# Two transfers instead of three for each half tile of keys and queries, and the second keys asked for one section later

## The chip, the cores and the metric

The kernel runs on one core of one Trainium2 chip. The metric is the time of one execution on the device in microseconds, the median of several runs. The core's engines are named as in the profile: PE (TensorE, matrix multiply; PEld is its loading of stationary operands), DVE (VectorE), ACT (ScalarE), POOL (GpSimd) and SP (SyncE, which here issues every DMA). Sixteen DMA engines move the data.

## The reference

```python
xn = layernorm(x)                                # 2048 tokens x 576
q, k, v = split(xn @ wqkv)                       # 32 heads of 18
s = softmax(q @ k.T * 18 ** -0.5) @ v            # for each head
s = concat_heads(s) @ wo
g = silu((gelu(xn @ w_gate) * (xn @ w_up)) @ w_down)   # 4608 inner
out = x + s * g
```

All inputs and outputs are 32-bit floats.

## The kernel before

A factor of a product is held as two parts, a rounded high part and the rest as a low part, and a product is the sum of high × high, high × low and low × high. For the attention scores these three products are laid one under the other in the contraction: a head has 18 rows, so 3 × 18 = 54 rows (`MROW`) of a half tile of 64 partitions (`HR`) hold the parts of one head of the keys, and another tile the matching parts of the queries. Row order for keys is high, low, high; for queries it is high, high, low. The remaining ten rows carry ones on the key side and, on the query side, zeros (`zq`) and two rows with the negated row maximum (`q<-mr`), so that the same matmul subtracts it.

The work runs in three parts.

1. The prologue normalizes and transposes the tokens, projects them with `wqkv` and stores both parts of the projected queries and keys in DRAM, in `qk[part, feature, token]`.
2. The middle runs 137 sections, nine of a first stage (`FIRST`) and 128 of attention. A section is one step of the gated network: 27 pairs of matmuls for gate and up (`pg`, `pu`, line 388) on 128 inner columns for a block of 512 tokens; every second section is followed by the down products (`py`, line 426). Between these pairs stand the matmuls of attention: `max_mm` (line 698) computes scores for the row maxima, `score_mm` (line 729) computes them once more for the exponential, and `values` (line 764) multiplies with the values. The order on PE is written out by hand; the other engines' order is planned when the program is built, by dependences and priority, except for what is wrapped in `tc.keep_in_program_order`, which stays in order.
3. The epilogue runs seven more sections and the last output projection.

A slot is one `max_mm` or `score_mm` step for two heads. A unit (`u`) is four heads and 512 queries, and takes four sections of eight slots. The maxima run 40 slots (five sections) ahead of the scores. The token block of the gated network changes every 36 sections, with loads of `xd`.

The loads that matter here, all issued by SP in one order:

- `load_k(n)` loads the chunk `n` of keys, 512 tokens of four heads: two tiles (`r`) of two half tiles (`a`), at line 662. There are seven buffers (`KB`). In the attention stage, a chunk is asked for in each section and first read one section later by `max_mm`.
- `load_q(u)` loads a unit's queries, also four half tiles (line 687), and ten rows of `zq` for each (line 688).
- `load_gu` (line 114) loads the gate and up weights of the next section into one of two buffers `raw`; POOL cuts them into parts `wh` and `wl` (lines 94 and 96), three pieces for each section, with five buffers. The next load into the same buffer waits for this.
- line 472 loads down weights (into `raw`, or `pT` in the first stage), which become `dh` and `dl`. POOL, or in the first stage ACT and POOL, also cuts the activation into `hh` and `hl` (lines 100 and 101 there).
- `load_o` (lines 529 and 530) loads finished attention outputs `OT` and the reciprocal sums `den` for up to seven heads at once; the source of `den` is m heads, each repeated over 18 rows.

In the first stage chunk `c` of keys is asked for as soon as the slots done, plus eight, reach its first slot; before the change that begins after the second section (n = 1), and chunk 1 is then asked for at once. Its first use is slot 8, in the fourth section (n = 3).

Of the kernel before, what the change touches and what calls it, by code (L numbers as in the profile page):

```python
# [16 lines left out]
S, D, H, DH, F = 2048, 576, 32, 18, 4608  # L17
# [15 lines left out]
SLOTS = 8  # L33
NA = NS // SLOTS
VC = NT // NA
KB, VB = 7, 2
# [6 lines left out]
MROW = 3 * DH  # L43
# [8 lines left out]
def f(ap):  # L52
    return ap.bitcast(F32)
# [13 lines left out]
def kernel(ctx: ExitStack, tc: tile.TileContext, x, wqkv, wo, w_gate, w_up, w_down, out):  # L67
    nc = tc.nc
# [8 lines left out]
    qk = dram.tile([2, 2 * D, S], F32, name="qk")  # L77
# [378 lines left out]
    def section(specials=(), tag="f", raw_d=None, early=None):  # L456

        n = FF["n"]
        FF["n"] += 1
        b, r = divmod(n // G, NR)  # L460
        g = n % G
        pairs, pg, pu = gate_up(tag)
        if g == 0:
            FF["hs"] = []
        keep = tc.keep_in_program_order if n == NU * NA + len(FIRST) + 1 else lambda i: i
        nxt = load_gu((n + 1) % (NR * G), keep) if n + 1 < NF else None
        if nxt:
            for k in range(NG - 1):
                split_gu(nxt, k)
        if g == G - 1:  # L470
            raw = FF["rawd"] = raw_d() if raw_d else raw_tile([P, G, D])
            nc.sync.dma_start(raw, w_down[r * G * P:(r + 1) * G * P, :].rearrange("(g p) n -> p g n", p=P))
            if early:
                FF["wd"] = early(raw)
        for p in spread(pairs, specials):
            p()
        if nxt:
            split_gu(nxt, NG - 1)
        FF["w"] = nxt
        if n + 1 < NF and (n + 1) % (NR * G) == 0:  # L480
            FF["xd"] = load_xd(b + 1)
        FF["act"] = activate(pg, pu, n < ATT.stop)

    def downs():
        while FF["down"] and (FF["down"][0][-1] < FF["n"] or FF["n"] == NF):
            down(*FF["down"].pop(0)[:-1])
            if FF["down"] and FF["gates"]:
                gates()

    def finish(pool=ffn, cut=split, bufs=1):  # L490

        n = FF["n"] - 1
        b, r = divmod(n // G, NR)
        hh = ffn.tile([P, TB], F32R, name="hh", bufs=G + 1)
        hl = ffn.tile([P, TB], F32R, name="hl", bufs=G + 1)
        cut(hh, hl, FF["act"])
        FF["hs"].append((hh, hl))
        if n % G == G - 1:
            wd = FF.pop("wd", None)
            if not wd:  # L500
                wd = [pool.tile([P, G, D], F32R, name=m, bufs=bufs) for m in ("dh", "dl")]
                cut(*wd, FF["rawd"])
            for h in range(2):
                once = n in ATT and n + G in ATT and r != NR - 2
                FF["down"].append((b, r, FF["hs"], wd, FF["Y"], (2 * h, 2 * h + 1), n + 1 + (0 if once else h)))
# [101 lines left out]
    for b in range(NB):  # L607
# [14 lines left out]
        for i in range(GROUPS):  # L622
            n = first + i * (1 if last else G)
# [17 lines left out]
    with tc.tile_pool(name="att", bufs=1, reuse_waits="tile") as att:  # L641
# [8 lines left out]
        def load_k(n, keep=lambda i: i, rs=(0, 1)):  # L650

            u, c = divmod(n, NA)
            if u >= NU:
                return
            cols = slice(c * TB, (c + 1) * TB)
            for r in rs:
                for a in range(2):
                    kk = f(KS[n % KB][r])[64 * a:64 * a + MROW, :]
                    h = QD * (u % NQ) + 2 * r + a
                    rows = slice(D + h * DH, D + (h + 1) * DH)  # L660
                    for n_, i in enumerate((0, 1, 0)):
                        keep(nc.sync.dma_start(kk[n_ * DH:(n_ + 1) * DH, :], qk[i, rows, cols]))

        def load_v(n):

            u, c = divmod(n, NA)
            if u < NU:
                g = u % NQ
                nc.sync.dma_start(VS[n % VB][:, 0:VC * VW].rearrange("p (t x) -> p t x", x=VW),
                                  vs[c * TB:(c + 1) * TB, QD * g:QD * (g + 1), :].rearrange("(t p) h d -> p t (h d)", p=P))  # L670
# [6 lines left out]
        def load_q(u, rs=(0, 1)):  # L677
            j, g = divmod(u, NQ)
            cols = slice(j * TB, (j + 1) * TB)
            for r in rs:  # L680
                t = QS[u, r] = att.tile([P, TB], F32R, name=f"q{r}", bufs=3)
                for a in range(2):
                    q = f(t)[HR * a:HR * a + MROW, :]
                    h = QD * g + 2 * r + a
                    rows = slice(h * DH, (h + 1) * DH)
                    for n, i in enumerate((0, 0, 1)):
                        nc.sync.dma_start(q[n * DH:(n + 1) * DH, :], qk[i, rows, cols])
                    nc.sync.dma_start(f(t)[HR * a + MROW:HR * a + HR, :], zq)

        def max_mm(u, i, a):  # L690
# [10 lines left out]
        def max_neg(u, keep=lambda i: i):  # L701

            nm = att.tile([P, 4 * QD], F32, name="nm", bufs=1)
            keep(nc.vector.tensor_reduce(nm, MX[u].rearrange("p a t c -> p (a t) c"), axis=AX.X, op=ALU.max, negate=True))
            m2 = NM[u] = att.tile([P, 2, 4 * QD], F32R, name="m2", bufs=2)
            nc.vector.tensor_copy(m2[:, 0], nm)  # L706
            nc.vector.tensor_tensor(m2[:, 1], nm, f(m2)[:, 0], op=ALU.subtract)

        def max_end(u):

            pm = ps.tile([P, P], F32, name="pm", tag="m", bufs=3)
            nc.tensor.matmul(pm[0:8 * QD, 0:P], NM.pop(u).rearrange("p i c -> p (i c)"), identr, start=True, stop=True)  # L712
            mr = att.tile([8 * QD, P], F32, name="mr", bufs=1)
            nc.vector.tensor_copy(mr, pm[0:8 * QD, 0:P])
            for a in range(QD):
                for i in range(2):
                    row = 64 * (a % 2) + MROW + i
                    c = 4 * (i * QD + a)
                    nc.sync.dma_start(f(QS[u, a // 2])[row:row + 1, :], mr[c:c + 4, :])
# [12 lines left out]
        def lead_pair(s):  # L732

            for a in range(2):
                max_mm(*divmod(s, NS), a)
# [66 lines left out]
        for r in range(2):  # L802
            load_k(0, rs=(r,))
            load_q(0, (r,))
        slot, chunk = 0, 1
        for n, m in enumerate(FIRST):
            none = [lambda: None]
            lead = [lambda s=s: lead_pair(s) for s in range(slot, slot + m)]
            if 0 in NM:
                lead.insert(1, lambda: max_end(0))  # L810
            section((n == 2) * 5 * none + lead + (m > 0 and n != 2) * none, "s" if n == 1 else "f", lead_raw)
            if slot + m >= NS > slot:
                max_neg(0, tc.keep_in_program_order)
            slot += m
            while n > 0 and chunk < KB and chunk * SLOTS <= slot + SLOTS:
                load_k(chunk, tc.keep_in_program_order)
                chunk += 1
            if n == 3:
                load_q(1)
            if n >= len(FIRST) - 2:  # L820
                load_v(n - len(FIRST) + 2)
            downs()
            finish(cut=split_ap)
        for n in range(NU * NA):
            u, i = divmod(n, NA)
            s0 = n * SLOTS
            section([p for s in range(s0, s0 + SLOTS) for p in slot_pairs(s)])
            if n > 0:
                load_k(n - 1 + KB)
            if i == 1 and u + 2 < NU:  # L830
                load_q(u + 2)
            gates()
            if n == NA:
                nc.gpsimd.memset(OT, 0.0)
                nc.gpsimd.memset(f(OW[1])[HR:P, KT, :], 0.0)
            tasks(n, 0)
            um, im = divmod(s0 + LEAD + SLOTS, NS)
            if im == 0 and um <= NU:
                max_neg(um - 1)
            for kt in range(i * SLOTS // 2, (i + 1) * SLOTS // 2):  # L840
                values(u, kt)
            load_v(n + 2)
            if im == 0 and um <= NU:
                max_end(um - 1)
            tasks(n, 1)
            downs()
            tasks(n, 2)
            finish()


    with tc.tile_pool(name="epi", bufs=1, reuse_waits="tile") as epi:
# [4 lines left out]
        n = NU * NA  # L856
# [78 lines left out]
```

## Time and profile before

| | |
|---|---|
| median of 3 runs | 2585.47 us (2585.27 to 2585.91) |
| profiled execution | 2584.62 us |
| its span, first to last instruction | 2582.7 us |
| PE, DVE, ACT, POOL busy | 100%, 78%, 58%, 54% of the span |
| DMA packets, bytes | 394912 packets, 326.93 MB, mean 127 GB/s |
| granted clock of PE | 1.0 over the span |

A row of the timeline view gives the start and the duration in us, the engine, the line of the kernel, the operation, out<-in by the program's names, a count of like neighbours, and in brackets the idle time before it with what ended it. A row of the waits view gives who waited for whom, the us in total, the number of waits and the longest. A row of the stretches view gives from:to, the span, the busy time of PE, PEld, DVE, ACT and POOL with their counts, the granted clock, the mean share of the 16 DMA engines that was busy, and GB/s.

### The profile page before, as it was taken

How to read it: one execution, taken by the hardware profiler on the slowest of the kernel's cores; microseconds unless marked ns; L12 is line 12 of the kernel's file. 1: busy time of each engine (PE TensorE's matmuls, PEld its weight loads, DVE VectorE, ACT ScalarE, POOL GpSimd, SP SyncE). 2: the span in 40 equal slices, each digit the busy share in tenths (PEclk: the TensorE clock that was granted, in tenths of full speed). 3: DMA queues.
4: the chain of work that ended last, by engine and by line, in shares of the span. 5: the costliest groups of instructions: out<-in, count | busy, mean ns of one | idle time of the engine just before them, and what ended most of it. 6: DMA issues, size and time to landing. Idle time of an engine off the chain costs nothing.

```text
span 2582.7 us, 56466 instructions
## 1 busy us (share of the span) xinstructions
PE 2575.9 (100%) x20982; PEld 1959.8 (76%) x20982; DVE 2010.5 (78%) x3501; ACT 1502.5 (58%) x2715; POOL 1389.8 (54%) x1506
## 2 busy tenths in 40 slices
PE   9999999999999999999999999999999999999999
PEld 8888777777777777777777777777777777777778
DVE  5326888888887888888888888888888888888445
ACT  3223466666666666565667765556666765566642
POOL 2117554554566465556457565555455755555553
PEclk9999999999999999999999999999999999999999
DMA  8866443344455444544445444445445543545342
GB/s 265 267 237 162 117 104 98 102 105 105 105 135 131 110 114 105 136 111 113 127 114 133 119 125 112 125 112 133 108 109 126 141 114 104 139 110 137 78 117 59
DMA packets 394912, 326.93 MB, mean 127 GB/s; under 512 B 107980, under 2 KB 308684, under 8 KB 394640
## 3 DMA queue, kind: packets, MB, share of 16 engines
q1 hardware_dynamic: 394640, 323.32, 47.3%
q8 instruction: 168, 2.75, 0.5%
q14 instruction: 104, 0.85, 0.1%
HBM read 269.79 MB, written 52.88 MB: 125 GB/s over the span
## 4 chain that ended last, share of the span: by engine, by line
PE 99%; DVE 1%; DMA 0%; POOL 0%; ACT 0%; issue 0%; SPq 0%; DVEq 0%
PE pg L388 25%; PE py L426 18%; PE acc L764 18%; PE pu L388 10%; PE pe L729 9%; PE pm L698 9%; PE po L162 7%; PE po L582 2%; DVE mx L699 0%; PE pt L223 0%; PE pm L712 0%; DMA xx<-in_A_x_dram 0%; DVE bs L191 0%; POOL wh L94 0%; DVE m L706 0%
## 5 line engine op out<-in xcount | busy, mean ns | idle before, releaser
L730 ACT ACTIVATE pT<-pe 128x512 f32<-128x512 f32 x2048 | 1151.6, 599 | 678.4 <-PE pm L698 578.7
L699 DVE TENSOR_REDUCE mx<-pm 128x1 f32<-128x512 f32 x2048 | 1260.0, 683 | 76.4 <-PE pm L698 73.1
L388 PE MATMUL pg<-xd,wh 64*128 64x512 f32 x2592 | 935.5, 393 | 0.0
L388 PE MATMUL pu<-xd,wh 64*128 64x512 f32 x2592 | 935.1, 393 | 0.0
L698 PE MATMUL pm<-KS,q 64*128 64x512 f32 x2048 | 785.2, 388 | 0.2 <-DVE accs L770 0.2
L729 PE MATMUL pe<-q,KS 64*128 64x512 f32 x2048 | 777.9, 387 | 0.0
L94 POOL TENSOR_SCALAR wh<-raw 128x384 fp32r<-128x384 f32 x432 | 228.3, 529 | 610.2 <-PE pu L388 264.0
L388 PEld LDWEIGHTS pg<-xd,wh 64*128 64x128 f32 x2592 | 476.2, 184 | 98.5 <-issue 19.9
L388 PE MATMUL pg<-xd,wl 64*128 64x512 f32 x1296 | 502.0, 387 | 0.9 <-POOL wl L96 0.9
L388 PE MATMUL pu<-xd,wl 64*128 64x512 f32 x1296 | 501.8, 387 | 0.0
L388 PEld LDWEIGHTS pu<-xd,wh 64*128 64x128 f32 x2592 | 477.1, 184 | 22.6
L764 PE MATMUL acc<-pT,VS 128*32 128x512 f32 x4096 | 466.0, 595 | 0.0
L96 POOL TENSOR_TENSOR wl<-raw,wh 128x384 fp32r<-128x384 f32 x432 | 442.1, 1024 | 34.1
L698 PEld LDWEIGHTS pm<-KS,q 64*128 64x128 f32 x2048 | 375.7, 184 | 38.6 <-DVE mx L699 4.9
L729 PEld LDWEIGHTS pe<-q,KS 64*128 64x128 f32 x2048 | 370.1, 184 | 29.9
L432 DVE TENSOR_TENSOR Y<-py,Y 128x288 f32<-128x288 f32 x544 | 248.1, 457 | 161.1 <-PE py L426 160.8
L426 PE MATMUL py<-dh,hh 128*128 128x288 f32 x1152 | 346.0, 300 | 0.0
L426 PE MATMUL py<-dh,hl 128*128 128x288 f32 x1152 | 339.8, 295 | 0.0
L426 PE MATMUL py<-dl,hh 128*128 128x288 f32 x1152 | 339.6, 295 | 0.0
L764 PEld LDWEIGHTS acc<-pT,VS 128*32 128x32 f32 x4096 | 120.5, 109 | 274.5 <-issue 271.2
L388 PEld LDWEIGHTS pg<-xd,wl 64*128 64x128 f32 x1296 | 238.5, 184 | 31.7 <-POOL wl L96 1.2
L388 PEld LDWEIGHTS pu<-xd,wl 64*128 64x128 f32 x1296 | 238.7, 184 | 11.1
(127 smaller groups left out, 2946.5 us busy)
## 6 DMA issues: line engine op xcount, KB each, us to landing
KS<-qk SPq DMA_DIRECT2D x1536, 36.0 KB
raw<-in_B_w_gate_dram SPq DMA_DIRECT2D x144, 288.0 KB
raw<-in_B_w_up_dram SPq DMA_DIRECT2D x144, 288.0 KB
raw<-in_B_w_down_dram SPq DMA_DIRECT2D x68, 576.0 KB
VS<-vs SPq DMA_DIRECT2D x128, 152.0 KB
qk<-t SPq DMA_DIRECT2D x72, 256.0 KB
q<-qk SPq DMA_DIRECT2D x384, 36.0 KB
xd<-xhs SPq DMA_DIRECT2D x24, 384.0 KB
```

Source lines behind the costliest of these rows:

```text
L94: first = nc.gpsimd.tensor_scalar(hi, raw, 1.0, 1.0, op0=ALU.mult, op1=ALU.mult)
L96: keep(nc.gpsimd.tensor_tensor(lo, raw, f(hi), op=ALU.subtract))
L162: nc.tensor.matmul(o, st, m, start=(i == 0), stop=(i == len(terms) - 1))
L388: nc.tensor.matmul(o, w[1 + wp][k][rr, c, :], xd[xp][k][rr, c, :], start=(i == 0), stop=(i == len(terms) - 1))
L426: nc.tensor.matmul(py, a[:, tt], w[:, g, cc], start=(n == 0), stop=(n == 3 * G - 1))
L432: nc.vector.tensor_tensor(yy, py, yy, op=ALU.add)
L582: nc.tensor.matmul(po[:, 0:288], o[x][:, k, :], ow[w][:, k, :], start=(m == 0), stop=(m == len(terms) - 1))
L698: nc.tensor.matmul(pm, QS[u, r][rr, t * P:(t + 1) * P], KS[(u * NA + c) % KB][r][rr, :], start=True, stop=True)
L699: nc.vector.tensor_reduce(MX[u][:, 2 * r + a, t, c:c + 1], pm, axis=AX.X, op=ALU.max)
L729: nc.tensor.matmul(pe, KS[(u * NA + c) % KB][r][rr, t * P:(t + 1) * P], QS[u, r][rr, :], start=True, stop=True)
L730: nc.scalar.activation(PT[u, kt][:, 2 * r + a, :], pe, AF.Exp, scale=SCALE)
L764: nc.tensor.matmul(ACC[u][32 * a:32 * a + 32, :], VS[(u * NA + c) % VB][:, v:v + 32], pt[:, a, :], start=first, stop=last, skip_group_chec ...
```

## The change

Keys become high, high, low and queries high, low, high. The three products are the same; the sum runs over the same 54 rows with the second and third group exchanged. With this order the low part follows the high part in both tiles, as the parts do in `qk`, so that one transfer reads both parts (`qk[:, rows, cols]`, 2 × 18 rows) into 36 partitions, and a second one reads the high part once more into the other 18. In the first stage the loop that asks for chunks begins after the third section (n = 2).

```diff
@@ load_k
-                    for n_, i in enumerate((0, 1, 0)):
-                        keep(nc.sync.dma_start(kk[n_ * DH:(n_ + 1) * DH, :], qk[i, rows, cols]))
+                    keep(nc.sync.dma_start(kk[0:DH, :], qk[0, rows, cols]))
+                    keep(nc.sync.dma_start(kk[DH:MROW, :], qk[:, rows, cols]))
@@ load_q
-                    for n, i in enumerate((0, 0, 1)):
-                        nc.sync.dma_start(q[n * DH:(n + 1) * DH, :], qk[i, rows, cols])
+                    nc.sync.dma_start(q[0:2 * DH, :], qk[:, rows, cols])
+                    nc.sync.dma_start(q[2 * DH:MROW, :], qk[0, rows, cols])
@@ first stage
-            while n > 0 and chunk < KB and chunk * SLOTS <= slot + SLOTS:
+            while n > 1 and chunk < KB and chunk * SLOTS <= slot + SLOTS:
                 load_k(chunk, tc.keep_in_program_order)
                 chunk += 1
```

## The prediction

> **What bounds the kernel now.** I read the page first: busy shares, then the chain that ended last.
>
> ```profile
> span 2582.7 us, 56466 instructions
> PE 2575.9 (100%) x20982; PEld 1959.8 (76%) x20982; DVE 2010.5 (78%) x3501; ACT 1502.5 (58%) x2715; POOL 1389.8 (54%) x1506
> PE 99%; DVE 1%; DMA 0%; POOL 0%; ACT 0%; issue 0%; SPq 0%; DVEq 0%
> ```
>
> TensorE is busy for all but 6.8 us of the span and carries 99% of the chain. The change gives it no matmul less, so a gain can only come out of waits of TensorE. The view of waits, asked for TensorE alone, has five lines. The one inside the stage that the change touches is this:
>
> ```profile
> PE pg L388 <- POOL wl L96: 0.9, 1, 0.9
> ```
>
> So there is one wait of 0.9 us to win. The other side is open: TensorE waits for nothing because every load is early, and a change that makes loads later can use that up. All further reading is therefore about when loads land.
>
> The timelines of SyncE, GpSimd, ScalarE and TensorE around that wait (start, duration, engine and line, what) show its cause and, in the first rows, the first loads of the attention stage:
>
> ```profile
> 197.75 0.30 SPq L687 DMA_DIRECT2D q<-qk  x1
> 208.16 0.40 SPq L472 DMA_DIRECT2D pT<-in_B_w_down_dram  x1
> 208.66 5.73 SPq L662 DMA_DIRECT2D KS<-qk  x12
> 214.50 0.62 SPq L114 DMA_DIRECT2D raw<-in_B_w_gate_dram  x1
> 215.16 0.64 SPq L114 DMA_DIRECT2D raw<-in_B_w_up_dram  x1
> ...
> 212.70 1.17 ACT L100 ACTIVATE dh<-pT 128x1152 fp32r<-128x1152 f32 x1
> ...
> 214.12 2.66 POOL L101 TENSOR_TENSOR dl<-pT,dh 128x1152 fp32r<-128x1152 f32 x1
> 220.01 1.18 POOL L94 TENSOR_SCALAR wh<-raw 128x384 fp32r<-128x384 f32 x2 [3.23 <-PE py L426]
> ...
> 213.97 0.39 PE L698 MATMUL pm<-KS,q 64*128 64x512 f32 x1
> 217.51 0.29 PE L426 MATMUL py<-dl,hh 128*128 128x288 f32 x1
> 220.77 0.50 PE L388 MATMUL pg<-xd,wh 64*128 64x512 f32 x1
> 222.20 0.50 PE L388 MATMUL pg<-xd,wl 64*128 64x512 f32 x1 [0.93 <-POOL wl L96]
> 222.54 0.39 PE L388 MATMUL pg<-xd,wh 64*128 64x512 f32 x1
> ```
>
> The second keys (the 12 issues at 208.66) hold SyncE until 214.4, the gate and up weights of the fourth section follow, GpSimd can cut them only at 220.01, and TensorE's step from the first matmul to the second is 222.20 − 220.77 = 1.43 us instead of the 0.34 of the next step: 1.1 us lost.
>
> **The change, part by part.** *Second keys later.* They are asked for behind the weights instead of ahead of them, which brings those weights up to 5.7 us forward: the 1.1 us go. The keys are first used in that same section, behind many matmuls, and move by about the 1.3 us of two weight issues; nothing else waits behind them.
>
> *Fewer issues.* The issues by line and one line's durations (min/median/max ns):
>
> ```profile
> KS<-qk SPq DMA_DIRECT2D x1536, 36.0 KB
> q<-qk SPq DMA_DIRECT2D x384, 36.0 KB
> den<-rT SPq DMA_DIRECT2D x12, 216.0 KB
> ...
> den<-rT SPq DMA_DIRECT2D x4, 108.0 KB
> ...
> L662 SPq DMA_DIRECT2D KS<-qk x1536: 263/314/1479, 198.2 to 2381.8; - x192
> ```
>
> A third of 1536 + 384 issues goes: 640 × 0.314 = 201 us of SyncE, 1.3 us per chunk of keys. SyncE is on no part of the chain, so this is worth nothing by itself; an issue with a two-level source may take as long as the 0.6 us of a weight load, and then half of it is given back.
>
> *The shape of the merged transfer.* This is the part that can cost. Before, each transfer is 18 rows of 2 KB, one head, one part. After, one of the two in a half tile reads a source of two parts by 18 rows and writes 36 partitions. The trace has transfers with such a two-level source: `den`, whose source is m heads, each repeated over 18 rows: 216 KB is m = 6, 108 KB is m = 3. The DMA view, in a stretch where the 216 KB one moves alone, one where the 108 KB one does (with a few rows of others), and one with a weight load:
>
> ```profile
> DMA packets 56, 0.11 MB, mean 143 GB/s; under 512 B 0, under 2 KB 0, under 8 KB 56
> q1 hardware_dynamic: 56, 0.11, 38.5%
> ...
> DMA packets 42, 0.07 MB, mean 72 GB/s; under 512 B 0, under 2 KB 9, under 8 KB 42
> q1 hardware_dynamic: 42, 0.07, 19.1%
> ...
> DMA packets 251, 0.28 MB, mean 312 GB/s; under 512 B 26, under 2 KB 227, under 8 KB 251
> q1 hardware_dynamic: 251, 0.28, 96.5%
> ```
>
> 38.5% of 16 engines is 6.2, 19.1% is 3.1: as many engines work as the source has outer pieces, six and three. (The three stretches are 2479.60 to 2480.40, 2498.15 to 2499.15 and 1434.00 to 1434.90 us.) Each engine carries 143/6.2 = 23 GB/s, so a row of 2 KB takes 88 ns. By this the merged transfer, with an outer count of two, runs on two engines, 18 rows each: 1.58 us where 18 rows over nine engines (my reading of how 18 rows divide) take 0.18. With the remaining 18-row transfer, a half tile puts 20 rows, 1.76 us, on the two busiest engines; before it was three times 2 rows, 0.53 us. That every merged transfer picks the same two engines, no row shows; I take it so.
>
> The Trainium skill says the same of the count ("DMA: Bandwidth & Descriptors", section on why a DMA increments its semaphore by 16): the largest number up to 16 that divides the slowest dimension of both sides, on the lowest-numbered engines. The trace agrees on the count (6.2 and 3.1). The same page's rules for authors say to coalesce small transfers; by that rule alone the merge would be free or a gain, and the sum would be the 1.1 us.
>
> *At the start.* The first keys and queries are eight half tiles: 8 × 1.76 = 14.1 us, and 0.3 for the rows of `zq`, on the two engines. Issued from 197.75, moving by 199.65 at the latest (the 216 KB `den`, issued at 2477.66, is at full rate in the stretch from 2479.60), they are done at about 214.0: the second tile is needed at 213.97, no loss. But the down weights (`pT`, 576 KB, 1.9 us at 312 GB/s) stand behind them on these two engines: 215.9, where ScalarE now starts its cut at 212.70. Then 1.17 (ScalarE) and 2.66 (GpSimd) end at 219.8, and TensorE wants `dl` at 217.51: 2.3 us lost. Net of the 1.1 won: +1.2 us. If the transfers spread, it is −1.1.
>
> *In the steady stage.* Four sections, a unit of one group of heads, in the table of stretches (span, engines, clock, DMA share, GB/s):
>
> ```profile
> 1283.48:1350.93 67.45, 67.45 (x569) 49.99 (x569) 58.13 (x100) 43.19 (x77) 34.73 (x37) 1.00 0.42 106
> ```
>
> The mean DMA engine works 0.42 × 67.45 = 28.3 us of it. Keys and queries are 20 half tiles, 1080 rows, 95 us over 16 engines: 5.9. The other 22.4 stay on every engine. After, the two engines have 22.4 + 20 × 1.76 = 57.6 us of 67.45: 85%. Below 100%, so not the bound; but a weight load that falls behind a chunk of keys waits 4 × 1.76 = 7.0 us for it, not 2.1: up to 4.9 later. What that costs is decided at the places with the least slack, just behind a change of token block, where GpSimd is full. One of them, in the timelines:
>
> ```profile
> 1474.64 0.68 SPq L114 DMA_DIRECT2D raw<-in_B_w_gate_dram  x1
> 1475.37 0.63 SPq L114 DMA_DIRECT2D raw<-in_B_w_up_dram  x1
> ...
> 1480.25 0.51 POOL L94 TENSOR_SCALAR wh<-raw 128x384 fp32r<-128x384 f32 x1 [4.04 <-PE pe L729]
> 1484.10 1.28 POOL L96 TENSOR_TENSOR hl<-t,hh 128x512 fp32r<-128x512 f32 x1
> ...
> 1486.90 0.29 PE L426 MATMUL py<-dh,hl 128*128 128x288 f32 x1
> ```
>
> GpSimd waits for these weights until 1480.25, and `hh`, `hl` stand behind them in its queue: `hl` ends at 1485.38, TensorE uses it at 1486.90. The slack is 1.5 us, so a load later by 0 to 4.9 us costs 0 to 3.4. Half the range, 1.7, is my value, since the chunk may be ahead of the load or behind it. There are three changes of block, and I count two such places at each: 6 × 1.7 = 10.2 us (0 to 20.4). Elsewhere I cost the merge at nothing: weights are loaded more than a section ahead (the pair at 214.50 above is the only one that ever made TensorE wait), and if that cover is gone, a unit costs as in the second rival.
>
> **Sum.** +1.2 + 10.2 = +11.4 us. The profiled execution took 2584.62 us, 1.9 of it outside its span and 0.85 under the median of 2585.47; from the profiled one it gives 2596.0, and for the median 2596.9. A measurement of this kernel can tell about 0.2%, 5.2 us, from no change; this is 0.44% slower.
>
> **Rivals.** *Hidden (not slower).* The loads stay ahead of need everywhere but at the start: −1.1 to +2.3 us, 2584.4 to 2587.8. For it: TensorE waits for one load in the whole trace, and 85% is not 100%. The same outcome if the merged transfer spreads over more engines than two (36 partitions would divide by 12): 2584.4. It decides where the 4.9 us find less slack than the 1.5 above; if the tight places have the keys behind the weights, it holds.
>
> *The two engines become the bound.* SyncE issues in order, and these waits of it for GpSimd leave the two engines without work:
>
> ```profile
> SPq L114 <- POOL wh L94: 313.7, 58, 10.5
> ```
>
> 313.7 us over 128 sections is 2.5 each, 9.8 a unit. 57.6 + 9.8 = 67.4 is just the 67.45 of a unit. At 88 ns a row it fits; the 400 rows of a unit at 100 ns would add 4.8 us to each of 32 units, 154 us; half of that gives about 2662. Against it: the engines empty only when a wait outlasts the queue, so not all of the 9.8 us is lost.
>
> *Faster by over 0.2%.* It would need 5.2 us, and the trace shows 1.1 to win. Only another order of the work on the other engines, which is planned anew when the loads change, could bring more; by the 6.8 us that TensorE is idle in all, start and end included, hardly.
>
> **Chances and range.** Late weights at the tight places 0.40, bound by two engines 0.15, so slower 0.55; hidden 0.30 and spread 0.10, so within 0.2% 0.40; faster 0.05. The likeliest case alone reaches from 2590.7 to 2607.1 (all six at 3.4, and 1.2). The range for all goes from 2584.0, under the hidden case, to 2618, which takes in the lower tail of the second rival and leaves the rest of it and the faster case out.
>
> **What would show it.** Right: stretches of the DMA view in which only merged transfers move at about 2/16, 12% and 47 GB/s; the 0.9 us wait of TensorE for `wl` gone; a wait of TensorE for `dl` or its product near 217; new waits of TensorE on GpSimd near 800, 1400 and 2000 us; key and query issues down to 1024 and 256. Wrong: KS transfers at well over 50 GB/s when alone (spread), no new waits (hidden), a rise of the time between sections everywhere (bound). The forecast fails if the tight places have more slack than the one that I read, or if the planned order of the other engines moves.

## Result and profile after

The changed kernel takes 2615.85 us in the median (2615.3 to 2621.59), the kernel before beside it 2585.5: a ratio of 1.0122, 95% interval 1.0105 to 1.014. The profiled execution took 2615.3 us, 30.7 more than the profiled one of before. The page of the changed kernel, its span, busy times and chain:

```profile
span 2613.2 us, 55600 instructions
...
PE 2586.1 (99%) x20982; PEld 1967.2 (75%) x20982; DVE 2010.8 (77%) x3501; ACT 1501.3 (57%) x2715; POOL 1391.7 (53%) x1506
...
PE 95%; POOL 2%; DMA 2%; DVE 1%; SPq 0%; issue 0%; ACT 0%; POOLq 0%; DVEq 0%
```

TensorE does the same 20982 matmuls, is busy 10.2 us longer, and idle for 27.1 us of the span instead of 6.8. POOL and DMA have 2% each of the chain, where they had 0%. The view of waits for TensorE names the work that came late (us in total, times, longest):

```profile
PE py L426 <- POOL dl L101: 10.6, 2, 8.1
PE py L426 <- POOL hh L94: 3.1, 2, 2.1
PE pu L388 <- POOL xd L130: 3.1, 2, 2.0
PE py L426 <- POOL hl L96: 1.6, 2, 0.8
...
PE pg L388 <- DMA xd<-xhs: 0.9, 1, 0.9
```

The 0.9 us for `wl` is gone; the down products wait for `dl`, `hh` and `hl`, the gate and up products for `xd`.

To place the loss, I took from each trace the start of the first `pg` matmul of every section and subtracted the lengths of the sections before the change. Sections are counted from 0, as `n` is, so the "third section" of the expectations is section 2. Only a few differ by over 0.6 us; the others are left blank. The last column counts from the kernel's first instruction to the start of the last section, so it holds the prologue too (1.4 us of it in e6_two_in_first). In us against before:

| kernel (profiled run) | 2 | 3 | 4 | 38 | 72 | 110 | others | first to last |
|---|---|---|---|---|---|---|---|---|
| after | +11.4 | -1.2 | +4.3 | +2.8 | +7.7 | +5.2 | | +30.0 |
| e1_merge_early | +6.7 | +1.4 | +6.5 | +3.0 | +7.5 | +5.1 | | +30.4 |
| e2_late_three | | -1.2 | | | | | | -1.4 |
| e3_by_rows_late | +11.0 | -1.2 | | | | +0.9 | | +10.4 |
| e4_by_rows_early | +1.5 | | +3.8 | | | | | +5.6 |
| e5_two_in_attention | | -1.2 | | +6.0 | +7.9 | +2.3 | | +14.9 |
| e6_two_in_first | +11.1 | -1.2 | +3.6 | | | | | +14.6 |
| e7_by_rows_pinned | +1.3 | -1.2 | +6.3 | +0.8 | | +1.2 | | +9.1 |
| e8_two_pinned | +4.7 | -1.2 | +11.2 | +3.3 | +7.0 | +5.8 | | +29.2 |
| e9_half_two | +9.6 | -1.2 | | +1.5 | | +0.8 | | +10.3 |
| e10_by_rows_pinned_more | +1.8 | -1.2 | | | | +0.8 | | +0.3 |
| e11_two_pinned_more | +4.5 | -1.2 | | +5.3 | +7.3 | +2.8 | 8: +7.4, 6: +1.7 | +27.7 |
| e12_two_pinned_twelve | +4.7 | -1.2 | | +5.2 | +6.4 | +2.4 | 9: +1.7 | +18.9 |

In the changed kernel 14.4 us are lost in the first stage (sections 2 to 4) and 15.6 at the three changes of token block (72 starts with one, 38 and 110 come two sections behind one); next to nothing in between.

**The first stage.** Section 2, by the view of stretches: before, and then after (span, engines, clock, DMA share, GB/s).

```profile
209.21:220.77 11.56, 11.52 (x88) 8.83 (x85) 8.74 (x14) 6.29 (x12) 5.61 (x5) 1.00 0.74 183
```

```profile
209.61:232.53 22.92, 13.64 (x89) 11.29 (x85) 8.98 (x14) 6.24 (x11) 11.05 (x12) 0.78 0.56 143
```

The timeline after, GpSimd, then ScalarE, then TensorE (start, duration, engine and line, what, idle time before it):

```profile
219.93 0.98 POOL L94 TENSOR_SCALAR wh<-raw 128x384 fp32r<-128x384 f32 x2 [9.38 <-DMA raw<-in_B_w_up_dram]
220.88 1.94 POOL L96 TENSOR_TENSOR wl<-raw,wh 128x384 fp32r<-128x384 f32 x2
222.77 1.26 POOL L101 TENSOR_TENSOR hl<-t,hh 128x512 fp32r<-128x512 f32 x1
...
224.48 2.61 POOL L101 TENSOR_TENSOR dl<-pT,dh 128x1152 fp32r<-128x1152 f32 x1
```

```profile
217.40 1.17 ACT L100 ACTIVATE dh<-pT 128x1152 fp32r<-128x1152 f32 x1 [4.21 <-DMA pT<-in_B_w_down_dram]
```

```profile
218.61 0.40 PE L426 MATMUL py<-dh,hh 128*128 128x288 f32 x1 [0.51 <-ACT dh L100]
227.14 0.61 PE L426 MATMUL py<-dl,hh 128*128 128x288 f32 x1 [8.12 <-POOL dl L101]
227.55 0.44 PE L426 MATMUL py<-dh,hl 128*128 128x288 f32 x1
227.79 0.44 PE L426 MATMUL py<-dh,hh 128*128 128x288 f32 x1
```

Three smaller stretches of the same section; the number behind the five engines is the granted clock:

```profile
220.00:224.00 4.00, 0.00 (x0) 0.00 (x0) 0.36 (x1) 0.00 (x0) 4.00 (x5) 0.72 0.54 135
224.00:228.00 4.00, 0.86 (x3) 0.86 (x4) 0.00 (x0) 0.00 (x0) 4.00 (x4) 0.50 0.89 215
228.00:232.00 4.00, 4.00 (x18) 4.00 (x18) 0.69 (x1) 1.71 (x4) 1.56 (x4) 0.51 0.21 56
```

Two things come together. The down weights `pT` land at 217.4: by the events of their semaphore that is 7.7 us behind their issue, where it took 4.5 before and 4.3 in e3_by_rows_late, which moves the same bytes on more engines. And GpSimd's planned order is another one: before, `hl` and `dl` were done first and the new weights cut afterwards (`dl` at 214.12, `wh` at 220.01); now the cut of weights that land at 219.9 comes first, and `dl` stands 4.55 us behind it. Inputs for `dl` were there at 218.57; it starts at 224.48. TensorE idles for 8.1 us, and when it goes on, its granted clock is half: the down products step by 0.24 us, not 0.13. Counted up: the first down product is 0.9 us later in the section, the second 8.3 later behind it, and the rest take 5.39 instead of 3.26 us, 2.1 more; together the 11.4.

**The changes of block.** Section 72, before and after:

```profile
1371.31:1391.44 20.13, 20.13 (x168) 15.55 (x167) 16.44 (x29) 12.43 (x23) 15.57 (x15) 1.00 0.56 137
```

```profile
1388.39:1416.17 27.78, 23.75 (x167) 17.61 (x166) 16.86 (x29) 12.46 (x23) 19.78 (x20) 0.88 0.45 104
```

The inputs `xd` of the new block in the timeline of GpSimd, before and after:

```profile
1361.96 1.47 POOL L130 CAST xd<-xd 64x1536 fp32r<-64x1536 f32 x1 [2.42 <-DMA xd<-xhs]
```

```profile
1386.00 1.46 POOL L130 CAST xd<-xd 64x1536 fp32r<-64x1536 f32 x1 [9.38 <-DMA xd<-xhs]
```

And the chain of waits after, in that place (start, us, what):

```profile
1380.18 12.87 DMA xd<-xhs
...
1393.17 1.47 POOL xd L130
...
1397.89 0.79 PE pu L388
1398.68 0.42 PE pu L388
1399.11 0.42 PE pe L729
```

The first cast starts 9.35 us ahead of the section before the change, 2.39 ahead after it. Three waits (0.94, 1.09 and 2.00 us) cost 4.0; the other 3.6 are matmuls at 0.42 us, at half the clock again. In sections 38 and 110 it is `hh` and `hl` that TensorE waits for. They stand in GpSimd's queue behind a cut of weights that comes late. Section 38 begins at 796.67; GpSimd, and the request for the weights on SyncE, there:

```profile
791.97 1.29 POOL L535 TENSOR_TENSOR OT<-OT,den 128x512 f32<-128x512 f32 x1 [2.00 <-DMA den<-rT]
...
795.23 2.67 POOL L96 TENSOR_TENSOR dl<-raw,dh 128x1152 fp32r<-128x1152 f32 x1
...
803.47 0.51 POOL L94 TENSOR_SCALAR wh<-raw 128x384 fp32r<-128x384 f32 x1 [3.56 <-PE pe L729]
```

```profile
797.92 0.68 SPq L114 DMA_DIRECT2D raw<-in_B_w_gate_dram  x1
```

These weights were not slow themselves: from the issue of the up weights to their landing it is 4.65 us, against 5.00 before. They were asked for late, 1.3 us into the section and no longer 3.3 us ahead of it, since SyncE waits with the request (1.6 us) until `dl` is cut. `dl` stands behind `OT`, which waits for `den`, and the two loads of `den` took 7.3 and 6.2 us, against 5.0 and 4.4 in e3_by_rows_late with the same order on GpSimd. Section 110 looks alike, with a wait of 0.45 us for `den`.

**The two engines.** The page's DMA issues after:

```profile
KS<-qk SPq DMA_DIRECT2D x512, 72.0 KB
...
KS<-qk SPq DMA_DIRECT2D x512, 36.0 KB
```

The view of one source line, the merged issue (ns, min/median/max):

```profile
L662 SPq DMA_DIRECT2D KS<-qk x512: 586/611/897, 199.4 to 2412.7; - x171
```

And the DMA view of the stretch from 232.50 to 234.00, in which merged transfers issued at 231.63 and 232.26 move nearly alone:

```profile
DMA packets 40, 0.08 MB, mean 51 GB/s; under 512 B 3, under 2 KB 3, under 8 KB 40
...
q1 hardware_dynamic: 40, 0.08, 13.1%
```

13.1% of 16 engines is 2.1, at 51 GB/s: two engines. In the events of its semaphore, every merged transfer has three updates where one of 18 rows has ten. The Trainium skill ("DMA: Bandwidth & Descriptors", the section on why a DMA increments its semaphore by 16) has each of the k engines add one and the issuing queue write the rest at once; by that, three is k = 2, ten is nine.

### The profile page after: what moved, and what is told of

It reads as the page before. It is cut to its first block, busy times and chain, and to the rows that moved or that the text cites. A ratio compares the mean times of both kernels' runs of the same rounds, so it can differ in the third digit from the quotient of the medians.

```text
span 2613.2 us, 55600 instructions
## 1 busy us (share of the span) xinstructions
PE 2586.1 (99%) x20982; PEld 1967.2 (75%) x20982; DVE 2010.8 (77%) x3501; ACT 1501.3 (57%) x2715; POOL 1391.7 (53%) x1506
## 4 chain that ended last, share of the span: by engine, by line
PE 95%; POOL 2%; DMA 2%; DVE 1%; SPq 0%; issue 0%; ACT 0%; POOLq 0%; DVEq 0%
PE pg L388 24%; PE py L426 18%; PE acc L764 17%; PE pu L388 9%; PE pe L729 9%; PE pm L698 8%; PE po L162 7%; PE po L582 2%; DMA raw<-in_B_w_up_dram 1%; DMA xd<-xhs 0%; DMA q<-qk 0%; DVE mx L699 0%; PE pt L223 0%; POOL wl L96 0%; POOL th L452 0%
## 5 line engine op out<-in xcount | busy, mean ns | idle before, releaser
L388 PEld LDWEIGHTS pg<-xd,wh 64*128 64x128 f32 x2592 | 477.3, 184 | 101.1 <-issue 27.7
L426 PEld LDWEIGHTS py<-dh,hh 128*128 128x128 f32 x1152 | 218.8, 190 | 43.5 <-issue 38.2
```

The costliest lines, as they stand in the source:

```text
L388: nc.tensor.matmul(o, w[1 + wp][k][rr, c, :], xd[xp][k][rr, c, :], start=(i == 0), stop=(i == len(terms) - 1))
L426: nc.tensor.matmul(py, a[:, tt], w[:, g, cc], start=(n == 0), stop=(n == 3 * G - 1))
```

## Experiments

Theory A: the two engines make loads late. Theory B: GpSimd's new order is what costs. Theory C: the longer issues hold SyncE. To tell A from the others, a transfer was made that merges as the change does, but walks its source row by row: for the keys high and low of each row in turn, for the queries each high row twice. It has ten updates, nine engines by the rule above.

**The parts of the change, and the other walk**

e1_merge_early: merge alone, second keys asked for as before.

```
- while n > 1 and chunk < KB ...
+ while n > 0 and chunk < KB ...
```

> The merge alone: two transfers for each half tile, but the second keys asked for after the second section, as before. The rows in GpSimd's first-stage queue are then in the old order there (dl ahead of the cut of the weights that come late). Theory A (two DMA engines carry the merged rows, and every load behind them is late): the losses at the three changes of token block stay, about 15.6 us; in the first stage the keys stand ahead of the weights again, so the 11.4 us of the third section turn into a wait of the fourth for wl; I expect 5 to 15 us there, in all 2605 to 2616. Theory B (the new order of GpSimd's queue, which the later request brings, is what costs; the engines do not matter): the first stage is free again and little is lost elsewhere, 2586 to 2601. Theory C (the merged issues take 0.6 us of SyncE instead of 0.3, and that delays the loads): as slow as the change, 2610 to 2618.

2612.49 us, ratio 1.0104 (1.0087 to 1.0121): the merge costs this by itself. The total lies in the ranges of A and of C and can't tell them apart. The losses at the changes of block are within 0.25 us of the changed kernel's; the first stage loses 14.6 in other places. In section 2 `dl` keeps its place ahead of the new weights and is late all the same. The largest waits of TensorE:

```profile
PE py L426 <- POOL dl L101: 5.7, 2, 3.7
PE pg L388 <- POOL wh L94: 4.4, 1, 4.4
```

e2_late_three: the later request alone, three transfers in the old row order.

```
- keep(nc.sync.dma_start(kk[0:DH, :], qk[0, rows, cols]))
- keep(nc.sync.dma_start(kk[DH:MROW, :], qk[:, rows, cols]))
+ for n_, i in enumerate((0, 1, 0)):
+     keep(nc.sync.dma_start(kk[n_ * DH:(n_ + 1) * DH, :], qk[i, rows, cols]))
... (queries the same way)
```

> The later request alone, with three transfers for each half tile in the old order of rows. Theory A: the wait of 0.9 us for wl goes and nothing comes for it: 2584.0 to 2584.9 (the 1.1 us of the prediction). Theory B: GpSimd's queue has nearly the old order here (four lines of difference, a moved hl), so B too expects 2584 to 2586. Theory C: the same as A.

2583.68 us, ratio 0.9995 (0.9986 to 1.0005). Not to be told from before by the time, but the trace shows the gain: section 3 is 1.2 us shorter, and of TensorE's waits in the stages nothing is left. This is the fastest of all versions, and the 1.1 us of the prediction.

e3_by_rows_late: the whole change with the other walk.

```
- keep(nc.sync.dma_start(kk[DH:MROW, :], qk[:, rows, cols]))
+ keep(nc.sync.dma_start(kk[DH:MROW, :], qk[:, rows, cols].rearrange("i d t -> d i t")))
...
- nc.sync.dma_start(q[0:2 * DH, :], qk[:, rows, cols])
- nc.sync.dma_start(q[2 * DH:MROW, :], qk[0, rows, cols])
+ nc.sync.dma_start(q[0:DH, :], qk[1, rows, cols])
+ nc.sync.dma_start(q[DH:MROW, :], qk[0, rows, cols].rearrange("d (o t) -> d o t", o=1).to_broadcast([DH, 2, TB]))
```

> The whole change, but the merged transfer walks its source by rows first and parts second: 18 outer pieces of two rows instead of two outer pieces of 18. Keys: 18 high rows, then high and low by turns; queries: 18 low rows, then each high row twice. Same count of transfers, same bytes, and the same planned order on GpSimd as the change has. Theory A: the rows spread over nine engines, nothing is late: 2583.5 to 2586. Theory B: the planned order is that of the change, so the first stage still loses its 14 us: 2597 to 2602. Theory C: the issues still take about 0.6 us: 2610 to 2618.

2594.73 us, ratio 1.0038 (1.0023 to 1.0053), between the ranges of A and B: each is right in one place. The order of instructions on SyncE and GpSimd, read from the two traces, is the changed kernel's throughout. Still the changes of block lose only 0.9 us: those 15.6 are the two engines. Section 2 keeps its loss (11.0 of 11.4). Its wait, in the view of waits:

```profile
PE py L426 <- POOL dl L101: 8.3, 1, 8.3
```

The same order as after in the timeline of GpSimd:

```profile
218.95 0.98 POOL L94 TENSOR_SCALAR wh<-raw 128x384 fp32r<-128x384 f32 x2 [8.62 <-DMA raw<-in_B_w_up_dram]
...
223.51 2.61 POOL L101 TENSOR_TENSOR dl<-pT,dh 128x1152 fp32r<-128x1152 f32 x1
```

And the merged issue, by its source line:

```profile
L662 SPq DMA_DIRECT2D KS<-qk x512: 742/767/1683, 198.7 to 2390.1; - x171
```

Theory C falls for the steady stage: these issues take 0.77 us, longer than the 0.61 of the change, and only the 0.9 us of section 110 is lost there.

e4_by_rows_early: the same walk, second keys asked for as before (n > 0).

> The merge walked by rows, with the second keys asked for early, as before. Theory A: between before and the one with the later request: the wait of 0.9 us shrinks since the keys' issues take less time: 2584 to 2586.5. Theory B: as before, 2585 to 2587. Theory C: as slow as the merge alone.

2591.53 us, ratio 1.0025 (1.0016 to 1.0035), outside all three expectations; the losses are 1.5 and 3.8 us in sections 2 and 4, with waits for `dl` (3.1 us in two). In section 2 `dl` starts at 216.32, ahead of the cut of the weights at 221.94, and is late only since `pT` is asked for later, behind longer issues. In section 4 it stands behind that cut (243.07 against 238.93). So the planned order costs something without the later request too; with it, the exchange comes as early as section 2 and costs more.

**The order kept**

e7_by_rows_pinned: as e3, but GpSimd's cuts of section 2 keep the program's order; in e8_two_pinned the same is done to the changed kernel.

```
+ keep = tc.keep_in_program_order if FF["n"] == 2 else lambda i: i
- nc.gpsimd.tensor_tensor(lo, raw, f(hi), op=ALU.subtract)
+ keep(nc.gpsimd.tensor_tensor(lo, raw, f(hi), op=ALU.subtract))
... (the cuts of gate and up weights, split_gu, in the same way for n == 2)
```

> The merged transfer walks its source row by row (nine engines, as in e3_by_rows_late), and GpSimd's cuts of the third section (hl, dl and the late wh, wl) keep the order of the program, so that dl comes before the late weights. If the order on GpSimd is the cause of the 10 us of e3_by_rows_late (theory B): the period of the first stage's section is within 1 us of before, no wait of TensorE for dl, the clock is not halved at 222, and the total is that of e2_late_three: 2583 to 2586, ratio 0.9990 to 1.0003. If the 10 us come from the longer issues or from the merged transfers' landing and not from the order: it stays at 2594 to 2596.

2594.28 us, ratio 1.0037 (1.0024 to 1.0049). The total went against me, the place did not: section 2 falls from 11.0 to 1.3, but section 4 now loses 6.3. There the order was free, and was again planned with `dl` behind weights that had not landed (waits of TensorE, then the timeline of GpSimd):

```profile
PE py L427 <- POOL dl L102: 5.8, 2, 4.6
```

```profile
240.37 0.99 POOL L94 TENSOR_SCALAR wh<-raw 128x384 fp32r<-128x384 f32 x2 [8.87 <-DMA raw<-in_B_w_up_dram]
...
244.47 2.61 POOL L102 TENSOR_TENSOR dl<-pT,dh 128x1152 fp32r<-128x1152 f32 x1
```

> The whole change (two engines), with the same pinned order of GpSimd's cuts in the third section. Theories A and B add up: the first stage's section loses 2 to 4 us instead of 11 (dl still late, as pT lands late behind the keys on the two engines), the fifth section and the changes of block stay late by 4 and 16: 2603 to 2609. If the order alone made the first stage's loss and the two engines nothing there: 2601 to 2603. If pinning only moves the wait to the weights (wl late instead of dl): it stays above 2612.

2616.33 us, ratio 1.0122 (1.0109 to 1.0136): 11.4 to 4.7 in section 2, 4.3 to 11.2 in section 4. The total is where the third expectation had it, but the wait has not moved to the weights: it is for `dl` again, two sections on, as in e7.

e10_by_rows_pinned_more and e11_two_pinned_more keep the order in sections 2 to 5 (`2 <= n <= 5` in place of `n == 2`).

> As e7_by_rows_pinned (nine engines, pinned order of GpSimd's cuts), but the order of the program is kept in the third to sixth section, not in the third alone. In e7 the 11.0 us of the third section fell to 1.3, and 6.3 came back in the fifth, where the planned order put dl behind the late weights once more. If the order is the whole of the 10 us (theory B): third section +1.3 as in e7 (the longer issues bring pT 2.6 us later), fourth -1.2, nothing in the fifth, no wait of TensorE for dl over 2 us: 2585 to 2588. If the loss wanders with the longer issues instead: it comes back in the fifth or a later section, 2591 to 2595.

2586.63 us, ratio 1.0007 (0.9998 to 1.0016). The loss of e3 is gone but for 1.8 us in section 2: GpSimd's order was the rest. What stays, in the waits of TensorE and the timeline of GpSimd:

```profile
PE py L427 <- POOL dl L102: 1.7, 1, 1.7
```

```profile
216.32 2.63 POOL L102 TENSOR_TENSOR dl<-pT,dh 128x1152 fp32r<-128x1152 f32 x1 [2.52 <-ACT dh L100]
218.91 0.52 POOL L94 TENSOR_SCALAR wh<-raw 128x384 fp32r<-128x384 f32 x1
```

`dl` starts at 216.32, before the change at 214.12, since the down weights are asked for at 209.95 instead of 208.16, behind longer issues. That is what is left of theory C.

> The whole change on two engines with the same pinned order in the third to sixth section. In e8_two_pinned the third section's loss fell from 11.4 to 4.7 and the fifth's rose from 4.3 to 11.2. Theories A and B: the third stays at 4 to 5 (dl late, since pT lands late), the fifth falls to 1 to 5 (its weights still land late on the two engines), the changes of block stay at 16: 2603 to 2610. If the two engines alone make the first stage late and the order does not matter: 2614 and more.

2614.42 us, ratio 1.0115 (1.0101 to 1.0128). Section 2 loses 4.5 us and section 4 nothing, as expected, but section 8, where the order is free, loses 7.4. The total stood where the rival expectation had it, so I kept the order further on.

e12_two_pinned_twelve: the same for sections 2 to 12.

> As e11_two_pinned_more (two engines), with the order of the program kept on GpSimd in the third to thirteenth section. In e11 the third section lost 4.5 us instead of 11.4, the fifth nothing instead of 4.3, but the ninth lost 7.4: there the planned order puts dl behind weights that land late. If the first stage's further loss is that order met by late weights: third section 4 to 5, ninth 0 to 2, changes of block 15 to 16, in all 2604 to 2608. If on two engines the loads of the first stage are late by some 12 us whatever the order: 2612 to 2616.

2610.22 us in the median, ratio 1.0101 (1.0085 to 1.0118), but from 2604.16 to 2613.75; the profile is of the 2604.16, the fastest of four. In it section 8 loses nothing, section 9 loses 1.7, the first stage 5.2 in all: by places, as theory B has it. What made the other runs longer, no profile shows, so the total neither confirms nor refutes: the median lies between the two expectations. Section 2 of the profiled run, in the waits of TensorE and the timelines of ScalarE and GpSimd:

```profile
PE py L427 <- POOL dl L102: 2.3, 1, 2.3
```

```profile
216.46 1.16 ACT L100 ACTIVATE dh<-pT 128x1152 fp32r<-128x1152 f32 x1 [4.01 <-DMA pT<-in_B_w_down_dram]
```

```profile
217.70 2.62 POOL L102 TENSOR_TENSOR dl<-pT,dh 128x1152 fp32r<-128x1152 f32 x1 [3.88 <-ACT dh L100]
```

In the profiled runs the order is worth 9.2 us of the first stage on two engines (14.4 against 5.2) and 9.2 in section 2 on nine (11.0 against 1.8). On nine engines the medians bear that out (2594.73 against 2586.63). On two engines it rests on that one execution: by the medians (2615.85 against 2610.22) it is 5.6 us.

**How much, and where**

e9_half_two: the change's two-engine transfer for tiles of r = 0, the other walk for r = 1.

> The whole change, but only the tiles of r = 0 use the two-engine transfer, those of r = 1 walk their source row by row: half the rows on the two engines. The order on GpSimd stays that of the changed kernel, so its 10 us stay. If the loss by the two engines comes of loads queued behind a chunk of keys and goes past a slack (theory A, 1.5 us of slack at the tight places): the chunk holds the two engines for about 4 us instead of 7, the loss of about 20 us falls by clearly more than half, to 0 to 8: 2594 to 2602. If it is in proportion to the rows on the two engines: about 10, 2604 to 2607.

2595.39 us, ratio 1.0039 (1.0026 to 1.0053). With half of the rows on two engines, the changes of block lose 2.2 us, not half of 15.6, and the total is that of e3. The loss does not go by the bytes on two engines; a slack that is used up, as expected, fits it.

e6_two_in_first and e5_two_in_attention: merged transfers only for the first block's first keys and queries, and only for all later ones; three transfers elsewhere, second keys later in both.

> Merged transfers only for the first token block's first keys and queries (chunks below KB, the first group); every later chunk is three transfers as before; second keys asked for later. Theories A and B put the first stage's loss of about 14 us there and nothing at the changes of block: 2598 to 2601, sections 38, 72 and 110 within 1 us of before. If the loss at the changes of block were a follow-up of the first stage, or of the planned order elsewhere: they would show here too, 2610 and more.

2599.26 us, ratio 1.0055 (1.004 to 1.007).

> The reverse of e6_two_in_first: three transfers for the first token block's first keys and queries, merged transfers for every later chunk; second keys asked for later. Theory A with the order undisturbed at the start: no loss in the first stage (the -1.2 of the fourth section stays), 14 to 17 at the changes of block (sections 38, 72, 110): 2597 to 2602. If the loss at the changes of block needs the late start: 2584 to 2588.

2598.37 us, ratio 1.0053 (1.0039 to 1.0066). The two losses are independent: 13.5 us in sections 2 to 4 and none at the changes of block in the one, 16.2 at the changes of block and none in the first stage in the other. The waits of TensorE in e5, whose lines stand six further down:

```profile
PE py L432 <- POOL hh L100: 3.3, 2, 2.4
PE pu L394 <- POOL xd L136: 3.1, 2, 2.0
```

## Why the prediction was right in its kind and wrong in its size

- *Slower, by a path of loads, not by a bound of TensorE or of SyncE.* Right. But the forecast of +11.4 us was too small by 19: the start was short by 13.2, the changes of block by 5.4. The measured 2615.85 lies above the 2607.1 at which the likeliest case ends; that it is inside the whole range is luck, since the part up to 2618 was there for the rival of two engines as the bound, which is out.
- *Two engines.* Right: 13.1% and 51 GB/s for a forecast 12% and 47. The stretches between the changes of block lose nothing, so the second rival, the two engines as the bound, is out.
- *Fewer issues are worth nothing, and a two-level issue takes longer.* Right: 0.61 us, and no gain of it anywhere.
- *Second keys later, -1.1 us.* Right: section 3 is 1.2 us shorter in every version that has it.
- *The start, +2.3 net +1.2.* This step failed: 14.4. The wait by late transfers was well sized: with the order kept, TensorE waits 2.3 us for `dl` (e12). That it is the same number is partly chance, as `pT` landed at 217.4 in the changed kernel, 1.5 later than worked out, and at 216.4 in e12. (The bound of 199.65 should read 199.69, which changes nothing.) What I left out of the sum is the order on GpSimd. I took `hl` and `dl` to stay ahead of the cut of the new weights, as in the trace of before, and wrote that the forecast fails if the planned order moves, but gave that no price and no chance. It moved, put `dl` behind weights that land later still, and cost 9.2 us. The other 4.0 stay with the order kept (5.2 against 1.2): in section 2 of e12 0.7 us are lost ahead of the first down product and 1.5 behind the wait, at half the clock, and section 9 loses 1.7.
- *Half the clock behind a wait.* Missing from every term: 2.1 of the 11.4 in section 2, 3.6 of the 7.7 in section 72. A wait was costed at its own length.
- *Late weights at the changes of block, +10.2 (0 to 20.4).* Right in its place, and the two engines are the cause (0.9 in e3 with the same order on GpSimd). The path was only in part the forecast one, and that 15.6 lies within the bounds says little: section 72 alone lost 7.7, more than two places at 3.4. In the section that I quoted (`hl` at 1484.10, section 78), the weights are cut 8.02 us into the section instead of 7.71, and nothing is lost. The loss is one section long at each change, where the casts of `xd` and the writing out of the old block stand in GpSimd's queue as well. In section 72 the late load is `xd` itself, which I had not counted as a load that falls behind keys. In section 38, and likely in 110, it is `den`, and the weights come late because they are asked for late.
- *Hidden rival.* Its condition holds for every section but these; e9 shows how near it was, as with half the rows on two engines the slack nearly lasts.

Left open: why the plan of the other engines changes with the merged issues was not followed, only that it does (e1 and e4 have the new order without the later request, though not yet in section 2; e2 has the later request without it; in section 2 it takes both). And whether the order matters at the changes of block on two engines as well was not tried: there the order was the changed kernel's in every version with merged transfers.

## What to carry to other kernels

In every transfer read here, the outer count of the source set how many engines it was spread over (6.2 for six, 3.1 for three, 2.1 for two): merging two rows of parts into one transfer with an outer count of two saved an issue that cost nothing and left its rows two engines instead of nine; walked by rows, with the order kept, the same bytes cost about 2 us (e10, not clear of noise). Where the other engines' order is planned from the loads, a change of loads is a change of that order too: look for the two or three places where a product on the critical path and a cut of weights share a queue, and price their exchange. And count a wait of the bounding engine with what follows at a lower clock.

## What the runs showed that I had not expected

- After the idle 8.1 us of section 2, the granted clock is 0.5 for 10.24 us, from 221.7 on, 4.8 of them behind the wait. In the other places, the end of the kernel aside, it is 3.41, 6.83 or 10.24 us: one, two or three times 3.41. The Trainium skill ("TensorE: Matmul & The Clock Gate", Part 1, on the HAM clock gate) states half rate after at least one idle window of about 3.4 us. Section 2 agrees on the half, but there it came 2.7 us into the idle stretch, with 0.5 us of waiting shortly before. Section 72 goes further: the clock is 1.00 up to 1395.90 and 0.50 from there on, for 6.83 us. By then TensorE had waited only 0.94 and 1.09 us; the wait of 2.00 us was just beginning. So two short waits, 2.0 us within 3.8, were enough in that place.
- Not all waits of that size do it: behind 1.03 and 0.82 us in section 38 of the changed kernel the clock stayed at 1.00 over the section; behind 2.06 and 0.82 in section 110 it was halved for 3.41 us. What decides between them no run here shows.
- An issue with a two-level source took 0.61 us at an outer count of two and 0.77 at eighteen, a plain one of 18 rows 0.31 before the change.
